# Gated attention and a Hyena block on one Trainium2 core: casts issued one by one behind squares, 64x64 matmuls throughout a batch's Q steps, all engines' orders in one script

## The chip, the cores and the metric

The kernel runs on one core of a Trainium2 chip. The metric is the device time of one execution in microseconds (us). The engines are TensorE (PE, its weight loads PEld), VectorE (DVE), ScalarE (ACT), GpSimd (POOL) and SyncE (SP). POOL and SP mostly issue DMA transfers here.

## The reference

For 8 batches of S = 3136 rows, with u and v of 256 columns and z of 64, all float32:

```python
scores = (1.0 / S) * np.matmul(z, z.transpose(0, 2, 1))
x = u * np.matmul(np.maximum(scores, 0.0) ** 2, v)      # gated attention
...
proj = x @ w_proj                                       # 256 x 768
x1, x2, x3 = proj[..., :D], proj[..., D:2*D], proj[..., 2*D:]
X2 = np.fft.rfft(x2, n=S, axis=1)
H = np.fft.rfft(filter_fft, n=S, axis=0)[None, :, :]
y = x1 * np.fft.irfft(X2 * H, n=S, axis=1) * x3
out = y @ w_out
```

## The kernel before

The inputs are cast to bf16 on their way in; sums are float32 in PSUM.

**Chunks.** The columns of each batch's score matrix are cut into seven chunks (512 five times, 256, 320), 56 chunks in all. A chunk's work on PE is a row of steps. S: scores of a block from zT (`score_mm`, L1650), as two 64-row matmuls at once. ACT (L1808) or DVE (L1810) takes the relu into R_t, and ACT (L1817) or DVE (L1819) squares it into A_t. W and v: the two halves of weighing v_t by A_t into ps_o_t (`by_rows`, L472). The score matrix is symmetric, so some blocks come from earlier chunks' A_t by DMA transposes on SP: M_t, M2e_t and M2o_t (L1757). At a chunk's end DVE multiplies ps_o_t by uT_t into xT_t (the xT eviction, L1861), uT_t being u transposed by SP (L1457).

**Projection and convolution.** A and a are projections, first DFT stages and the like, also through `by_rows`. T is a small table of cosines and sines, made on DVE at the start (gs_t, L811 to L794). Evictions of PSUM by copy are L512 on ACT and L516 on DVE. The convolution is an FFT of length 3136 = 64 x 49. Its middle is the Q steps (`quads`, L1044), sixteen for a batch, whose matmuls are 64x64: forward with S, inverse with TZ, spectra in xh and spec_in_t. B, G and Z steps lead in and out of it (gates in gate_t, products in yT_t, results in ost_t).

**Forms.** A matmul's tile on PE is 64*128 (contraction by output rows) or 64*64; two of the first or four of the second fill the array. `by_rows` and `score_mm` emit 64x128, or two 64x64 in its place when `plan.quarters` is set. Before, `forms()` sets it for an S, W or v that stands between two adjacent Qs of the order, and for Qs.

**Order.** The kernel is unrolled in Python and a `Plan` chooses when each task is emitted. Each engine executes its instructions in the order of emission. PE's order is the string `ORDER`, one letter for a step. Which of ACT and DVE does a relu, square or copy is the string `ENGINES`. All else (what ACT, DVE, SP and POOL do next, which of the three PSUM pairs a step takes, how many fillers PE gets) is decided by `Plan` from assumed costs. Fillers (L674) are matmuls of the identity whose result nobody reads; they keep PE active.

**Casts.** POOL loads the next operands. In each chunk a copy of one element, `await_x` (tick, L561), makes POOL wait for the chunk's xT eviction; then all of that chunk's casts follow: in the first three chunks a third of the filter (xh, L645; the last with its last row, L650, and w_out, L651), z (zn_t, L552), v for the next batch (v_t, L571), and u for two chunks on (un_t, L552). The z and u casts are transposed by SP, `load_uT` (L1457) being added at the xT eviction.

The opening: z of the first batch is loaded (L588), cast into xT_t (L516), transposed on PE (L713), copied to zT_t (L512 or L516), and the first scores follow.

Of the kernel before, what the change touches and what calls it, by code (L numbers as in the profile page):

```python
# [20 lines left out]
NJ = 16  # L21
CHUNKS = (512, 512, 512, 512, 512, 256, 320)
INF = float("inf")
# [4 lines left out]
CLOG = 4.6  # L28
SLOW_TO = 9.0
FILL, SPARE = 0.23, 0.35  # L30
OPENING, AWAKE = 10.5, 7
SPEC_LAG = 1
LATE_F = 3.0
LATE_OUT = 1.5
# [3 lines left out]
TURN = 0.235  # L38
REACH = 2
SHARE = {0: 1, 2: 3}  # L40
SWITCH = 0.096


ORDER = (
    "ASSASSSWWvSAWAWSvSvSvWSWWSvSWvSvWSvWWSvSWvWSvvSSSWSvWWWWWAWavSvAWWSWBvWSvSavWvWSSvvvvvBBaAaaWSWWAWSavWWWAAav"
    "aSWWSWSvvAvavSWSvAWWavSvSvvvBSSWABWavSWWWBSSvavvvBSWWWWaWSWSvvWvvSvASWaSvBvaSWvSWAWWWWWaBWaSvWvWWSvAvvSSavWv"
    "BvaSWvASaSAAaavvSSAaWWWWWWSSvvvWWAASvvaWvWaAvvvQSaWWWSWWWAAavWavWvQWSQvvWSSvWWSvAWavvSvvSvAaSSSWWWSvWvAWvSvW"
    "aSWWWSSvAvavAvWSSWWaWQSvQvvSvQASaWWWSWSSvWAWaWvSvWWSvSSvWSvAvWAWaSvWavSvvvQQAaWSWSvWSAWaWQSvWQWWWSQvSvvvWWQv"
    "QWWvSQvvvvASAaaWWQQvWvSWWSQvWvSWSvWQQvvWvSWQWQWWSvvQvSvAAaaWWQWWSQvAvavSWWSvSvWSvSAvaSWWWWASvSWavSWSvSAvavAB"
    "aaAWWavvWASWaASWaAvvWaBWvaWBWSavvSvSWSBvBaaAWavSBWaWWASvaWASWvWvSWavSWWWSBWSavvWASvavvvvABSaaWWAWaASvaSWAvaA"  # L50
    "WAaaWSvWSvWSvvSAvSaWSWWBSvvWaBWvSavvSSBaSWWWWSWSSvWvvvWSSWBvWWWSSvaWWSBvvaAvaSvSvvAQAaWaWWSWSAWWSavWQvSvvvvS"
    "SSWWWWSWWQvSvAvvvvAaSaWWWQWQvvWQSSWvvWWWQQvWvWSSvSvWWvSQvQvvAAaSaWWWQQWWWSQvSvvSWQWvvWAWavSAvWWWvSvSavvSvAAa"
    "AaWaSWWWWWAWSavSvWQvSvWvvSWQSvvvSAAaSWavWWAWaSvvWWSSSWvWWASvvvSaWWWvWSSvvvAvBSaaWWSWSWWWBSvavSvWSvSWAvaAvSWa"
    "BWSvaAvaAWWaWSBvavAvvaAAaSaWSWWSvBAaaSWvWSSvWSWWASvaWvAvavBSWWavSBvaWWvSSvvABaaWBWWSaSvvWSWBSaWAvaSvvQQvWWWS"
    "WQAvaSvWvABaWaWQvSvQvAASaaWWWSSvWWSvAvaAvQWWQvSWWQvvWvQBaWaWSvWBSvaSvvAAaSaWWQSSvWWSvQQvvWQWWSWQvSvWvAWWSvaA"
    "vSvaQWWSvQvAASaaWWWWSvvSWvSBvWWWSavSvvSWABvSaWaAvaAAaWSavWWSSvWWSWvSSvWBvaWWWSWAWAaWvavvSASavvvvSABaaWWSSvvW"
    "BSWWSavBWWaAvaSvWSvWSAvSWWaWvAvSaSvWvSBvaBAaaSWWAWaWSSWSvWAWaAvavSWBaWSSWvWSvABaSavWvBWaAvSvavSvvBSaSWWQQSvv"
    "WWQvASWvWWaWBQvSaWvSvBWaQvQWWSvWQSvvvBAaaQWWSWQWWSQvWWQvSvQWWvSvWQQvAvaSvAWavAvBaWaSWQvQvAAaSaWWWWWSASvvSvSv"
    "WAaWSWWvaSvvSWWSAvaWBSWavSvBvaSBvaBAaaWAvWWWBSaavvWWSWAvSavvWSAWSaAWavSvSvBASaWWWBaavSWWWSvBvSBaaWWWWSAvaWvW"
    "SBvavvSWvAvAavavBSSaWWWSAvSavWvSSvWWWAAaSavSWvSWSAvAaWSWaSvWBBWaavvSvvSBSaSWWWSWASvvvavSWSWWWAvavSvQWQWWWSWv"  # L60
    "SSvvvvQASaWWQWWWSQvWWWQWQvWSAvSvaAvavvQWSSvWWSvQvSvvAAaSaWWWASaWQvvSQWSvvWQWWWWQWSAvvaWSWQvSvvSvQvvQAAaaSWWW"
    "WAWaSvSWvSvvSWASvavSWWvWASSvWvaWWBSavvvSABaaSWWWWSWWASvWSWaBvvvBaWvSWvaSvvvBASaWaWBvavSWWAWSaWAvavWSAvaWSvWW"
    "SSvWvWWvSAvavvBAaSaWWWASWaSvvWSWSvWSBWvSWaSvBWaWvSAvWSavSWAvSavSvvAAaaBWaSWWWSvWvASvWaWSBvWSavSWvSWWSvSvWWSS"
    "vvBvvaASaAWWWaSvWWSWvvSBvaWSvWSvQSWWWQvvSQvWWvQvvAAaaQWWQvQWSWWAvaWSAWaAWaSvSvvSvvSQWWQWWWSvQvSvAvavAAaaSWWW"
    "BSvavWQvWWQSvvQWSWQvWASvWWSvSavAWWvavvSASaAWWWavWSWWSvvSSvvQvSWWWSWQvvSvASAaaSWWWAWWaSvWWSWvSAWvWSavWvSvvWSv"
    "WvvSvvSASaWSWWWAvaWSWSvWAvSWavWSSvWBvavAvWBaWSavAvvaAWaSvABaaBWSWaAvWaWSAvSaSvWSWvSSvvWWWSAvSWWvSvvaWWSvvSAB"
    "aaBWWWavSWvSWSvSWWBvWaSvWWSvASvWaWSQWSvvQvSvvGAaBaaWWBSvaQWWWQvABvaWSavvQWQSvWWvSSvWWSWvSWQvQvvBAaaWWWSQSvWW"
    "QWWWSWSvWvQvSQvvWvSQvvWQWASvSvvaSAaQWWWWQvvWvWSWSWSWvBWaAvSvavSvvASSaWWWWWASvSaWvvvWWSvAWGvvWWWavWavvAvvaBGa"
    "aAGaaZAaaBGaaBZaaZGaBaaZBaaQQGQQBaQQQaQQBaBQQaQGZQQQaBaQGaGaZBaGaaaBaBaGBaBaaBaBGaBaaBaBGaaBaBBBaaaBa"
)  # L70
# [108 lines left out]
class Plan:  # L179
# [45 lines left out]
    def run(self, task, engine, start):  # L225
# [16 lines left out]
        if engine == "PE" and start < SLOW_TO:  # L242
            cost *= 2
# [1694 lines left out]
```

## Time and profile before

| | us |
|---|---|
| median of 3 runs | 949.24 |
| lowest, highest | 947.19, 952.63 |
| profiled execution | 947.53 |
| its span (first to last instruction) | 945.8 |

The busy shares of the span are PE 97%, DVE 88%, ACT 87%, POOL 21%. A "busy" PE is not PE at its peak: ends of matmuls are modelled, so how far apart the groups start tells more. In rows of a timeline, the bracket at the end is the idle time of the engine before the row and what ended it. The shapes of a matmul row are tile, then what moves through it, and the count after x merges equal neighbours.

### The profile page before, as it was taken

Reading aid. Unit: us, or ns where it says so; the run is one execution under the profiler, and the core shown is the slowest. Engines: PE = TensorE matmul, PEld = TensorE weight load, DVE = VectorE, ACT = ScalarE, POOL = GpSimd, SP = SyncE. Lnnn points to the kernel's source line nnn. Section 1 sums busy time; section 2 is a strip of 40 time slices with the busy share of each in tenths; the row PEclk is TensorE's granted clock in tenths of the full one; section 3 lists DMA queues with packets and bytes.
Section 4 is the critical chain, followed back from the end, with each engine's and each line's share of the span. In section 5 each row is a group of like instructions: output and inputs, shape, how many; then the busy total and the mean of one; then the engine's idle time right before and its main releaser. Section 6 shows DMA issues by size and latency. Waiting matters only on the chain.

```text
span 945.8 us, 29001 instructions
## 1 busy us (share of the span) xinstructions
PE 920.9 (97%) x11990; PEld 544.6 (58%) x11990; DVE 836.6 (88%) x1182; ACT 825.5 (87%) x927; POOL 200.8 (21%) x434
## 2 busy tenths in 40 slices
PE   8998999999999999999999999999999999999986
PEld 3443654557555775557655576556765566555754
DVE  8995699997999999999999779999889988799785
ACT  7785699998899898898989989999899999999672
POOL 5232303122213112212021120312212220001130
PEclk9998999999999999999999999999999999999999
DMA  9999678998999598998799998999899969798867
GB/s 152 152 176 153 146 135 161 176 191 177 181 198 173 110 209 173 207 206 165 156 208 191 204 201 175 183 178 187 173 168 187 190 124 182 172 201 143 210 204 243
DMA packets 321765, 168.40 MB, mean 178 GB/s; under 512 B 231990, under 2 KB 297334, under 8 KB 321632
## 3 DMA queue, kind: packets, MB, share of 16 engines
q1 hardware_dynamic: 290976, 128.39, 66.1%
q0 software_dynamic: 29616, 36.44, 26.1%
q8 instruction: 94, 1.54, 0.7%
q10 hardware_dynamic: 1040, 1.70, 0.6%
q14 instruction: 39, 0.32, 0.1%
HBM read 90.26 MB, written 53.35 MB: 152 GB/s over the span
## 4 chain that ended last, share of the span: by engine, by line
PE 81%; DMA 6%; DVE 6%; ACT 3%; issue 2%; SPq 2%; ACTq 0%; DVEq 0%
PE ps_o_t L472 48%; PE ps_s L472 20%; PE ps_s L1650 10%; PE ps_s L1044 3%; DMA spec<-gs_t 1%; DVE R_t L1810 1%; DMA M2e_t<-A_t 1%; DVE A_t L1819 1%; DMA spec_in_t<-spec 1%; DVE xT_t L1861 1%; ACT R_t L1808 1%; DMA specf<-s_t 1%; DMA ost_t<-in_z_dram 1%; DVE xh L1268 0%; DMA A_t<-spec 0%
## 5 line engine op out<-in xcount | busy, mean ns | idle before, releaser
L472 PE MATMUL ps_o_t<-A_t,v_t 64*128 64x512 bf16 (+4 forms) x4736 | 506.4, 354 | 0.6 <-DVE xT_t L1861 0.4
L472 PEld LDWEIGHTS <-v_t 64*128 64x128 bf16 (+1 forms) x6510 | 295.9, 98 | 209.6 <-PE ps_o_t L472 13.1
L1808 ACT ACTIVATE R_t<-ps_s 128x1024 f32<-128x1024 f32 (+4 forms) x353 | 332.1, 963 | 38.6 <-PE ps_s L1650 29.7
L1817 ACT ACTIVATE A_t<-R_t 128x1024 bf16<-128x1024 f32 (+3 forms) x283 | 276.0, 995 | 22.8 <-DVE R_t L1810 11.0
L1819 DVE TENSOR_TENSOR A_t<-R_t 128x1024 bf16<-128x1024 f32 (+4 forms) x209 | 229.7, 1116 | 15.2 <-ACT R_t L1808 12.8
L1810 DVE TENSOR_SCALAR R_t<-ps_s 128x1024 f32<-128x1024 f32 (+4 forms) x159 | 175.6, 1114 | 27.4 <-PE ps_s L1650 22.4
L1650 PE MATMUL ps_s<-zT_t 64*128 64x512 bf16 (+5 forms) x1209 | 190.9, 353 | 5.8 <-ACT R_t L1808 3.8
L561 POOL COPY tick<-xT_t 1x1 bf16<-1x1 bf16 x54 | 9.6, 178 | 636.5 <-DVE xT_t L1861 636.5
L472 PE MATMUL ps_s<-xT_t,wp 64*128 64x512 bf16 (+2 forms) x864 | 120.3, 349 | 0.5 <-ACT R_t L1808 0.4
L1650 PEld LDWEIGHTS <-zT_t 64*128 64x128 bf16 (+1 forms) x1209 | 68.0, 97 | 50.9 <-issue 6.6
L512 ACT ACTIVATE x_t<-ps_s 128x1024 bf16<-128x1024 f32 (+3 forms) x82 | 76.6, 943 | 19.8 <-PE ps_s L472 18.7
L472 PE MATMUL ps_o_t<-M_t,v_t 64*128 64x512 bf16 (+4 forms) x864 | 93.4, 352 | 0.0
L1861 DVE SCALAR_TENSOR_TENSOR xT_t<-ps_o_t,uT_t 128x256 bf16<-128x256 f32 (+2 forms) x224 | 71.3, 380 | 11.6 <-PE ps_o_t L472 5.8
L1268 DVE TENSOR_TENSOR xh<-xh,H 128x2048 bf16<-128x2048 bf16 x60 | 72.4, 1218 | 1.7 <-ACT xh L512 1.4
L1177 DVE TENSOR_TENSOR gate_t<-ps_s,x_t 128x512 bf16<-128x512 f32 (+2 forms) x106 | 60.6, 613 | 13.2 <-PE ps_s L472 9.0
L1365 DVE TENSOR_TENSOR yT_t<-ps_s,gate_t 128x1024 bf16<-128x1024 f32 (+2 forms) x52 | 56.3, 1087 | 12.7 <-PE ps_s L472 10.7
L472 PE MATMUL ps_s<-wp,xT_t 64*128 64x256 bf16 x800 | 65.3, 269 | 0.4 <-DVE s_t L516 0.2
L472 PEld LDWEIGHTS <-wp 64*128 64x128 bf16 x896 | 47.4, 94 | 30.2 <-issue 3.6
L552 POOL DMA_DIRECT2D un_t<-in_u_dram x112 | 59.7, 552 | 10.2 <-issue 6.8
L472 PE MATMUL ps_s<-wo,yT_t 64*128 64x256 bf16 x756 | 60.6, 270 | 0.9 <-DVE yT_t L1365 0.6
L571 POOL DMA_DIRECT2D v_t<-in_v_dram x112 | 58.8, 541 | 8.2 <-issue 7.0
L472 PE MATMUL ps_o_t<-M2e_t,v_t 64*128 64x512 bf16 (+2 forms) x440 | 52.0, 353 | 1.6 <-DVE xT_t L1861 1.5
(176 smaller groups left out, 881.0 us busy)
## 6 DMA issues: line engine op xcount, KB each, us to landing
out_dram<-ost_t SPq DMA_DIRECT2D x58, 256.0 KB
spec_in_t<-spec SPq DMA_DIRECT2D x56, 192.0 KB
spec<-gs_t SPq DMA_DIRECT2D x56, 192.0 KB
v_t<-in_v_dram POOLq DMA_DIRECT2D x80, 128.0 KB, 5.0
un_t<-in_u_dram POOLq DMA_DIRECT2D x80, 128.0 KB, 5.5
spec<-s_t SPq DMA_DIRECT2D x40, 256.0 KB
conv_in_t<-spec SPq DMA_DIRECT2D x34, 256.0 KB
out_dram<-ost_t POOLq DMA_DIRECT2D x10, 256.0 KB, 3.7
```

The costliest lines, as they stand in the source:

```text
L472: last = matmul(o[ds(i, n)], w[:, ds(i, n)], m, **kw)
L512: nc.scalar.activation(out_, in_, AF.Copy)
L552: nc.gpsimd.dma_start(out=t[ds(j * N1, N1), lo - t0 : hi - t0, :], in_=x[:, n2 : n2 + hi - lo, :])
L571: nc.gpsimd.dma_start(out=t[ds(j * N1, N1), ds(v_at(a), (b - a) * D)], in_=r[:, n2 + a - lo : n2 + b - lo, :].rearrange("p t d -> p (t d)"),)
L1177: nc.vector.tensor_tensor(g[:, :, ::-1] if h == 0 else g, p, x, ALU.mult)
L1268: nc.vector.tensor_tensor(x, x[:, 1].unsqueeze(1).to_broadcast([P, 2, 2, 2 * D]), h, ALU.mult)
L1650: matmul(o[ds(m, n)], zt[h, ds(t * P + m, n)], q, start=True, stop=True)
L1808: nc.scalar.activation(r, p, AF.Relu)
L1810: nc.vector.tensor_single_scalar(r, p, 0.0, ALU.max)
L1817: nc.scalar.activation(a, r, AF.Square)
L1819: nc.vector.tensor_tensor(a, r, r, ALU.mult)
L1861: nc.vector.scalar_tensor_tensor(x[:, ::-1] if h == 0 else x, f, inv_s2, ut, ALU.mult, ALU.mult)
```

## The change

One string, `SCRIPT`, replaces `ORDER`, `ENGINES` and the planner's costs. It holds PE's steps in order (a digit behind the letter for the PSUM pair and for which of the waiting tasks), and between them c, d, s and p with a number: the next task of ACT, DVE, SP and POOL by its place among the tasks that wait. `F` with two digits is that many fillers (second, in base 36) into a pair (first).

```diff
+SCRIPT = (
+    "d4d4d0d4F0oA00d4d3F12S1c0d2S2c2d2d2d2A00c3c2d3d2F13Wc1c1S1d0S2d2d1Wc0A00p0c0d1S1S2c1d1Wd1A00c0Wd2S1s0c0vd1S2"
...
```

The first line holds `F0o`, 24 fillers, ahead of the first transposes (`A00`). Eight more stand ahead of all, as before. Fillers are 44 in all (32 before): 8, 24, 2, 3 and, at the end, 7; before they were 8, 3, 4 and, at the end, 17.

The form of PE's tiles goes by spans, from the first to the last of a batch's sixteen Qs:

```diff
+    def spans(self, steps):
+        at = [i for i, x in enumerate(steps) if x[0] == "Q"]
+        cuts = [0, *range(len(at) % NJ, len(at) + 1, NJ)]
+        got = [False] * len(steps)
+        for a, b in zip(cuts, cuts[1:]):
+            for i in range(at[a], at[b - 1] + 1):
+                got[i] = True
+        return got
...
+        for (k, *x), self.quarters in zip(steps, self.spans(steps)):
```

In the built order the matmuls on PE grow from 11990 to 14133, and the places where neighbours differ between 64x128 and 64x64 fall from 92 to 20. DVE has 176 relus and ACT 336 (159 and 353 before), and of the copies DVE has 8 more and ACT 8 fewer.

The casts wait for squares and not for the xT eviction. A chunk's casts are put into `due`, and one is released behind each of the squares 1 to 5 of the next chunk, in the order u, v, z, filter; where POOL takes a released cast is set by `SCRIPT`. The filter comes in six parts (three before), v's cuts move by a row group, and `load_uT` is added with its cast:

```diff
+PACE = (1, 2, 3, 4, 5)
...
-    def await_x(xt):
-        nc.gpsimd.tensor_copy(tick[:], xt["t"][0:1, 1, 0:1])
+    def await_q(un):
+        tc.add_manual_dep(
+            nc.gpsimd.nop().ins, squares[un].ins.name, mybir.DependencyInfo(needs, reason.DATA), reason="paces the casts",
+        )
...
-    filt_cuts = ((0, 8), (8, 16), (16, NT))
+    filt_cuts = ((0, 4), (4, 8), (8, 12), (12, 16), (16, 20), (20, NT))
...
-            got.append(go_u)
+                load_uT(*slots[x], [])
+
+            got.insert(0, go_u)
+        got += late_
...
+        at_ = [u_ for u_ in scored if u_[:2] == un[:2]].index(un)
+        if at_ in PACE and due:
+            due.pop(0)(on("POOL", lambda un=un: await_q(un), 0.1, [q_]))
...
-            calls = casts_at(b, c)
-            if calls or b == 0 and c < 3:
-                tick_ = on("POOL", lambda xt=xt: await_x(xt), 0.1, [x_])
...
+            assert not due, (b, c, len(due))
+            due += casts_at(b, c)
```

POOL issues 378 DMAs for 356 before; SP's DMAs are as many as before. The line numbers shift by about 90 (by_rows 472 to 376, fillers 674 to 580, casts of u and z 552 to 456, of v 571 to 477, of the filter 645 to 551, M transposes 1757 to 1673).

How the instructions move, at three places. First DVE in the opening, from the first cast of z. Before (gs_t is the table T in the making, ps_s_139 the pair with the transposed z):

```order
L516 CAST xT_t<-ost_t 128x4x64 x2
L811 TENSOR_SCALAR gs_t<-yT_t,percol 128x32 x4
L812 TENSOR_SCALAR gs_t<-yT_t,percol 128x1
L813 TENSOR_SCALAR gs_t<-yT_t,percol 128x1
L789 TENSOR_SCALAR gs_t<-gs_t 128x128
L790 TENSOR_SCALAR gs_t<-gs_t 128x128
L516 CAST xT_t<-ost_t 128x8x64 x2
L794 SCALAR_TENSOR_TENSOR gs_t<-gs_t 128x128
L1810 TENSOR_SCALAR R_t<-ps_s_141 128x1024
L516 COPY zT_t<-ps_s_139 128x1024
```

After:

```order
L420 CAST xT_t<-ost_t 128x4x64 x2
L420 COPY zT_t<-ps_s_139 128x512
L717 TENSOR_SCALAR gs_t<-yT_t,percol 128x32 x4
L718 TENSOR_SCALAR gs_t<-yT_t,percol 128x1
L719 TENSOR_SCALAR gs_t<-yT_t,percol 128x1
L695 TENSOR_SCALAR gs_t<-gs_t 128x128
L696 TENSOR_SCALAR gs_t<-gs_t 128x128
L420 CAST xT_t<-ost_t 128x8x64
L700 SCALAR_TENSOR_TENSOR gs_t<-gs_t 128x128
L1726 TENSOR_SCALAR R_t<-ps_s_141 128x1024
L420 COPY zT_t<-ps_s_139 128x1024
```

The first zT eviction came from ACT and is now DVE's, ahead of the steps for T; one of the casts of 128x8x64 went to ACT.

Second POOL, at the casts of the third chunk of the first batch. Before:

```order
L561 COPY tick<-xT_t 1x1
L645 DMA xh_120<-in_moe_filter_fft_dram 64x8x256
L645 DMA xh_120<-in_moe_filter_fft_dram 64x2048
L649 MEMSET gate_t 64x256
L650 DMA gate_t<-in_moe_filter_fft_dram 64x256
L651 DMA wo_205<-in_moe_w_out_dram 128x2x256
L571 DMA v_t<-in_v_dram 64x1024 x2
L552 DMA un_t<-in_u_dram 64x1024 x2
L552 DMA zn_t<-in_z_dram 64x256 x2
L552 DMA zn_t<-in_z_dram 64x512
```

After (the waits for squares stand between them and are not among these rows):

```order
L456 DMA un_t<-in_u_dram 64x1024 x2
L477 DMA v_t<-in_v_dram 64x1024
L477 DMA v_t<-in_v_dram 64x256
L477 DMA v_t<-in_v_dram 64x1024
L477 DMA v_t<-in_v_dram 64x256
L551 DMA xh_120<-in_moe_filter_fft_dram 64x4x256
L551 DMA xh_120<-in_moe_filter_fft_dram 64x1024
L456 DMA zn_t<-in_z_dram 64x256 x2
L456 DMA zn_t<-in_z_dram 64x512
L551 DMA xh_120<-in_moe_filter_fft_dram 64x4x256
L551 DMA xh_120<-in_moe_filter_fft_dram 64x1024
L555 MEMSET gate_t 64x256
```

The burst behind one tick has become five releases, u first, with the filter in two parts (its last row and w_out follow). On SP around the same place, M2e_t before and after:

```order
L1757 DMA_TRANSPOSE M2e_t<-A_t 128x8x128
L1521 DMA_TRANSPOSE zT_t<-zn_t 128x4x128
L961 DMA spec_0_59<-s_t 128x4x256
L1457 DMA_TRANSPOSE uT_t<-un_t 128x8x128
L1757 DMA_TRANSPOSE M2e_t<-A_t 128x8x128
```

```order
L1673 DMA_TRANSPOSE M2e_t<-A_t 128x8x128
L1673 DMA_TRANSPOSE M_t<-A_t 128x8x128 x2
L1673 DMA_TRANSPOSE M2e_t<-A_t 128x8x128
L867 DMA spec_0_59<-s_t 128x4x256
L1363 DMA_TRANSPOSE uT_t<-un_t 128x8x128
```

The second M2e_t no longer stands behind a uT_t transpose, and the two M_t transposes stand between the two.

Third PE, behind a Q step in the middle of the kernel. Before:

```order
L1044 MATMUL ps_s_141<-spec_in_t,S_218 64x512
L472 LDWEIGHTS T_216
L472 MATMUL ps_s_139<-x_t,T_216 128x512
...
L472 LDWEIGHTS v_t
L472 MATMUL ps_o_t<-A_t,v_t 128x512
```

After:

```order
L950 MATMUL ps_s_140<-spec_in_t,S_218 64x512
L376 LDWEIGHTS T_216
L376 MATMUL ps_s_141<-x_t,T_216 64x512
...
L376 LDWEIGHTS v_t
L376 MATMUL ps_o_t<-A_t,v_t 64x512
```

The step behind the Q, and the weighing behind it, keep 64 output rows inside the span; before, the wide form came back at once.

More of the change, by code (lines that the diff above doesn't have):

```diff
@@ L264, in run @@
+    def run(self, task, engine):
+        task.emit(engine)
         for kid in task.kids:
-            for d, extra in kid.deps:
-                if d is task:
-                    kid.ready = max(kid.ready, end if extra == ISSUED else end + lat + (extra or 0.0))
             kid.left -= 1
```

363 lines of the change are left out of this document (133 added, 230 removed).

## The prediction

> **What bounds the kernel now.** I read the page first, then a table of stretches, then TensorE's timeline inside them. A run is told from no change when it moves by more than about 0.5% (4.7 us).
>
> ```profile
> span 945.8 us, 29001 instructions
> PE 920.9 (97%) x11990; PEld 544.6 (58%) x11990; DVE 836.6 (88%) x1182; ACT 825.5 (87%) x927; POOL 200.8 (21%) x434
> ...
> PE   8998999999999999999999999999999999999986
> ...
> PEclk9998999999999999999999999999999999999999
> ```
>
> TensorE (PE) is busy for 97% of the span, and the slices show where it is not: the first two, the fourth (the clock dips there too) and the last two. The stretches say the same in us (columns: length, then busy PE, PEld, DVE, ACT, POOL, granted clock, DMA share, GB/s).
>
> ```profile
> 12.00:30.00 18.00, 15.43 (x141) 6.41 (x138) 17.75 (x22) 16.59 (x18) 5.10 (x11) 1.00 1.25 152
> 60.00:70.00 10.00, 9.57 (x92) 4.03 (x89) 9.03 (x19) 9.38 (x10) 4.99 (x10) 1.00 1.09 140
> 70.00:80.00 10.00, 6.62 (x48) 2.76 (x46) 4.86 (x5) 3.83 (x4) 1.56 (x3) 0.77 1.41 166
> 80.00:90.00 10.00, 8.90 (x73) 4.04 (x71) 7.03 (x10) 5.49 (x6) 3.35 (x8) 0.88 0.79 133
> 100.00:850.00 750.00, 746.74 (x9849) 449.62 (x9849) 680.21 (x930) 688.32 (x774) 150.59 (x325) 1.00 0.95 178
> 900.00:946.00 46.00, 35.13 (x578) 21.79 (x572) 31.81 (x37) 24.97 (x27) 10.15 (x19) 0.96 0.73 221
> ```
>
> From 100 to 850 us PE idles 3.3 us of 750. There only less work on PE, or the same work at a better pace, saves time. Elsewhere a wait that goes is a gain, if nothing else ends late behind it. A delay of the opening reaches the end undiminished, since the long middle has no slack to take it up.
>
> **Part 1: the form spans.** A change between 64x128 and 64x64 matmuls is seen as a longer step from one group to the next (columns: start, length, engine, line, operation, tiles, shape, count).
>
> ```profile
> 303.75 0.61 PE L472 MATMUL ps_o_t<-A_t,v_t 64*128 64x512 bf16 x4
> 304.19 0.61 PE L472 MATMUL ps_o_t<-M2e_t,v_t 64*128 64x512 bf16 x4
> 304.73 0.41 PE L1044 MATMUL ps_s<-xh,TZ 64*64 64x512 bf16 x4
> 304.97 0.39 PE L1044 MATMUL ps_s<-spec_in_t,S 49*64 49x512 bf16 x4
> 305.19 0.60 PE L472 MATMUL ps_o_t<-M_t,v_t 64*64 64x512 bf16 x8
> 305.62 0.60 PE L472 MATMUL ps_o_t<-A_t,v_t 64*64 64x512 bf16 x8
> ...
> 309.07 0.39 PE L1044 MATMUL ps_s<-spec_in_t,S 49*64 49x512 bf16 x4
> 309.39 0.39 PE L472 MATMUL ps_o_t<-A_t,v_t 64*128 64x512 bf16 x2
> ```
>
> Start to start, four 64x128 matmuls take 0.44 us (303.75 to 304.19), and eight 64x64 ones 0.43 (305.19 to 305.62): the forms work at one pace. Into the Q step the four take 0.54 (304.19 to 304.73), so the change costs about 0.11. A Q group takes 0.22 between neighbours of its own form (304.97 to 305.19) and 0.32 into the wide form (309.07 to 309.39): 0.10. Another place reads higher, or has a record missing:
>
> ```profile
> 525.54 0.61 PE L472 MATMUL ps_o_t<-A_t,v_t 64*128 64x512 bf16 x3
> 526.08 0.41 PE L1044 MATMUL ps_s<-xh,TZ 64*64 64x512 bf16 x4
> ```
>
> 0.54 for three, 0.33 of work: 0.21. I take 0.11, the lower rows' value, since four in 0.54 would give the same. The instructions in order have 92 changes before and 20 after. Of these 74 and 17 lie between the places of 110 and 880 us, so 57 fewer: 57 x 0.11 = -6.3 us (bounds 57 x 0.10 = -5.7 and 57 x 0.21 = -12.0). The 2143 more matmuls are halves of wide ones and cost nothing at the pace above; the cover is that two run side by side. Some 38 groups of eight have only 128 columns, a case not in this trace: by columns 0.108 us each (a quarter of 0.43), at worst twice that, so 0 to +4.1; I take 0, the value to which 512 columns are nearest.
>
> This rests on the weight loads staying hidden:
>
> ```profile
> L472 PEld LDWEIGHTS <-v_t 64*128 64x128 bf16 x4538 | 234.0, 94 | 170.5 <-issue 13.0 <-PE ps_o_t L472 11.8 <-DVE xT_t L1861 9.4
> L472 PEld LDWEIGHTS <-v_t 64*64 64x64 bf16 x1972 | 62.0, 106 | 39.1 <-PE ps_o_t L472 1.3 <-PE ps_s L1044 1.0 <-DVE xT_t L1861 0.2
> ```
>
> A narrow load takes 106 ns for half the columns, a wide one 94: dearer, but beside the matmuls in both. The Trainium skill (TensorEngine Tiling (Array Packing), Restrictions) says that column tiling disables the fast weight load, which speaks against longer spans. The 106 ns agree with it in sign; the equal pace says that it is not felt.
>
> **Part 2: the casts.** The worst place of the kernel is one burst of them.
>
> ```profile
> 62.69 0.18 POOL L561 COPY tick<-xT_t 1x1 bf16<-1x1 bf16 x1 [10.82 <-DVE xT_t L1861]
> 63.15 1.23 POOL L645 DMA_DIRECT2D xh<-in_moe_filter_fft_dram  x2 [0.29 <-issue]
> ...
> 65.90 1.06 POOL L571 DMA_DIRECT2D v_t<-in_v_dram  x2
> 66.92 1.08 POOL L552 DMA_DIRECT2D un_t<-in_u_dram  x2
> ```
>
> Behind one xT eviction POOL queues the last third of the filter, then v, u and z. The chain of waits and the timeline go on:
>
> ```profile
> 63.93 10.68 DMA M2e_t<-A_t
> ...
> 74.69 1.06 ACT L1817 ACTIVATE A_t<-R_t 128x1024 bf16<-128x1024 f32 x1 [4.80 <-DMA M2e_t<-A_t]
> ...
> 76.71 0.58 PE L1650 MATMUL ps_s<-zT_t 64*128 64x512 bf16 x1 [3.38 <-ACT R_t L1808]
> 76.72 4.84 PE L472 MATMUL ps_o_t<-A_t,v_t 64*128 64x512 bf16 x20
> ...
> 86.96 1.28 PE L472 MATMUL ps_o_t<-M2e_t,v_t 64*128 64x512 bf16 x8 [1.04 <-DVE xT_t L1861]
> ```
>
> A transpose of squares that falls among these transfers is under way for 10.68 us. ScalarE's next square waits 4.80 for its buffer, the relu stands behind that square, and PE waits 3.38 for the relu. Then twenty matmuls take 4.84 us where 20 x 0.108 = 2.16 would do, at a granted clock of 0.77 and 0.88: 2.7 more. A last wait is 1.04. At stake: 3.38 + 2.68 + 1.04 = 7.1 us.
>
> After the change u comes first in that chunk, each cast stands behind its own early square, and the filter comes in halves among v and z. Both M2e transposes of the place now stand ahead of the next uT transpose on SP; before, the second stood behind one. But the same bytes move in about the same 10 us (squares 1 to 5 of a chunk surround the xT eviction), and M_t transposes come later in SP's queue. I take -5.0 of 0 to -7.1. The late thing next would be an M_t transpose, with the same form of wait.
>
> By the Trainium skill (TensorE: Matmul & The Clock Gate, Part 1) an idle gap of a window of about 3.4 us halves the clock. The 3.38 of wait with 0.77 behind it agree; by that rule a wait merely shortened to 2 us would give back 1.4 of itself and all 2.7 of the clock, -4.1.
>
> The other effects of this part are costed at 0. The 54 tick copies become POOL nops; 22 more DMAs at about 0.6 us of issue (1.23 for two) are 13 us on POOL. The cover is its idleness:
>
> ```profile
> L561 POOL COPY tick<-xT_t 1x1 bf16<-1x1 bf16 x54 | 9.6, 178 | 636.5 <-DVE xT_t L1861 636.5
> ```
>
> 636.5 us of waiting ahead of the ticks. A nop that waits for a square holds the next casts behind it, then SP's uT transpose and z's, needed about a chunk later; if that cover were gone, one late uT costs a wait like the 1.04 at 86.96. Load_uT issued earlier on SP moves uT ahead of some M transposes: 0, up to one such wait in each of a few chunks, which is inside the bounds of the stall.
>
> **Part 3: the opening.**
>
> ```profile
> 1.72 3.59 PE L674 MATMUL ps_s<-ident 128*128 128x512 bf16 x8 [1.72 <-DVE tick L598]
> ...
> 5.55 0.79 DVE L811 TENSOR_SCALAR gs_t<-yT_t,percol 128x32 f32<-128x32 int32 x4
> 5.69 0.61 PE L713 MATMUL ps_s<-ident,xT_t 128*128 128x128 bf16 x4 [0.37 <-DVE xT_t L516]
> ...
> 7.39 0.61 PE L1650 MATMUL ps_s<-zT_t 64*128 64x512 bf16 x4
> ...
> 9.18 0.68 DVE L516 COPY zT_t<-ps_s 128x1024 bf16<-128x1024 bf16 x1
> ...
> 9.92 0.82 PE L1650 MATMUL ps_s<-zT_t 64*128 64x512 bf16 x6
> ...
> 923.93 2.12 PE L674 MATMUL ps_o_t<-ident 128*128 128x512 bf16 x9
> ```
>
> Eight fillers at the slow clock take 3.59, the last of them 0.6 to its end: 0.43 apart. Nine at the full clock take 2.12: 0.21 apart. The clock is full by the scores at 7.39 (0.61 for four, as at 303.75). After the change 32 fillers stand ahead of the first transposes: 13 x 0.43 from 1.72 is 7.3, and 19 x 0.21 more is 11.3. The transposes start there and not at 5.69, though their data is there at 5.6. The first zT eviction moves from ScalarE to VectorE, ahead of the sine steps (from 5.55 in the rows), which so start near 12.2. From 5.55 to the second scores at 9.92 are 4.4 us, giving 16.6 and a lag of 6.7. The waits of 12 to 30 us (18 - 15.43 = 2.6) may take up part; I take +5.0, bounds +3.0 and +6.7.
>
> **Part 4: the tail and the engines.** After 900 us PE idles 10.9 of 46 and others end its waits. There 15 changes (1.65) and 10 fillers (2.1) are fewer, mostly inside waits: 0 to -3.8, taken -1.3. VectorE gets 17 more relus and 8 more copies, ScalarE as many fewer:
>
> ```profile
> L1810 DVE TENSOR_SCALAR R_t<-ps_s 128x1024 f32<-128x1024 f32 (+4 forms) x159 | 175.6, 1114 | 27.4 <-PE ps_s L1650 22.4
> ```
>
> 25 x 1.11 = 28 us more work on VectorE, 22 of them between 100 and 850. The cover is its idleness there, 750 - 680.2 = 69.8, of which 22.4 us in this row alone wait for PE: 0, with the case where the cover fails among the rivals.
>
> **The sum.** +5.0 - 5.0 - 6.3 - 1.3 = -7.6 on a profiled span of 945.8, so 938.2. That execution took 947.53, so 939.9; it was 1.7 below the median 949.24, which gives 941.6 for the median. I say 941, the full form saving being the lower of its readings. The bounds of the parts make it 922 to 954; both ends need all terms on one side.
>
> **Rivals.**
> - The stall stays, or moves to an M_t transpose: the filter's bytes are the same. For it speaks the DMA share of 1.41 in 70 to 80; against it that M2e leaves ahead of the casts. 941 + 5 = 946.
> - The opening is not felt: if the 2.6 us of waits from 12 to 30 and later small ones take up most of it, 941 - 4 = 937. Against it: PE is the last to be late from 100 on.
> - The changes of form are not what costs, the first load of a new kind of tile is: then 57 fewer give nothing, 947. Against it: within the Q spans tiles alternate too, at 0.22.
> - Slower: VectorE becomes the bound. From 100 to 850 it would have 702 us of work in about 743, idle 41. If its order needs more idle than that, PE waits for relus. At 55 idle the stretch is 757 and the time 955; at today's 69.8, 772 and 970. Against it speaks that its idle time is mostly ended by PE.
> - Slower: the narrow loads are felt in the longer spans. 2143 wide matmuls become 4286 narrow ones; at 12 ns each, two side by side, +26: 967. The equal pace at 305 speaks against it.
>
> **How the numbers follow.** Forecast 0.50 (own range 935 to 946), stall stays 0.15, opening not felt 0.13, VectorE 0.12, forms not the cost 0.07, loads felt 0.03. Faster (below 944.5): 0.43 of the forecast, 0.05 of the stall, 0.13, 0.02 of the forms: 0.63. Slower (above 954): three quarters of VectorE and the loads, 0.11. The rest, 0.26, is the same. The range 932 to 956 leaves out about 0.03 below and 0.11 above.
>
> **What would show it.** First scores near 13 and second near 16.6 in the opening; no PE wait of 3 us and no clock below 0.95 from 60 to 90; about 20 changes of form at 0.1; PE idle from 100 to 850 still under 5 us, VectorE near 94% there. I am wrong if PE waits for R_t or xT_t in the middle, if the early squares hold casts so long that uT is late, or if 64x64 passes in the spans run slower than 0.43 for eight.

## The result, and the profile after

The changed kernel takes 985.27 us (four runs, 981.45 to 990.31) against 948.76 for the kernel before on the same chip: a ratio of 1.038, 95% interval 1.031 to 1.045. The forecast was 941, so it is wrong in sign, and the time lies outside the range. The profiled run has a span of 988.5 us, 42.7 more than before. Below, the time of a run is the median of its executions in the fast state, where the record tells a slow one too.

The page of the kernel after (busy time, then the slices of TensorE and of its granted clock):

```profile
span 988.5 us, 33292 instructions
...
PE 933.5 (94%) x14133; PEld 604.5 (61%) x14133; DVE 858.8 (87%) x1205; ACT 808.8 (82%) x904; POOL 203.2 (21%) x402
...
PE   7999899899999999998998999899999899999976
...
PEclk9999999899999999999998999999999899999999
```

The dip of the fourth slice is gone. In its place six 8s stand in the middle, where before had none, and at three of them the clock dips as well. The stretches (length, then busy PE, PEld, DVE, ACT, POOL, clock, DMA share, GB/s) give the amounts:

```profile
12.00:30.00 18.00, 14.40 (x114) 6.40 (x114) 16.36 (x27) 13.54 (x18) 3.88 (x8) 0.91 1.32 159
60.00:70.00 10.00, 9.83 (x102) 4.79 (x98) 9.92 (x11) 7.67 (x8) 2.20 (x4) 1.00 1.25 191
70.00:80.00 10.00, 9.21 (x85) 4.10 (x85) 9.90 (x14) 6.00 (x7) 7.45 (x14) 1.00 1.14 170
80.00:90.00 10.00, 9.60 (x87) 4.16 (x83) 9.82 (x17) 6.59 (x9) 4.66 (x9) 1.00 1.30 209
100.00:850.00 750.00, 718.80 (x11195) 475.09 (x11196) 659.92 (x909) 638.71 (x713) 146.23 (x284) 0.98 0.95 168
900.00:988.50 88.50, 72.89 (x1335) 51.69 (x1323) 67.04 (x92) 55.37 (x67) 15.53 (x30) 0.97 0.71 197
```

From 60 to 90 us TensorE (PE) is busy 28.64 of 30, before 25.09, and at the full clock. From 100 to 850 it idles 31.2 us where before it idled 3.3, at a clock of 0.98. VectorE is idle for 90 us there: it is no bound.

The two traces can also be compared at the same work (columns of matmuls done by PE, fillers left out). The kernel after is 7.5 us behind at 30 us of before, 8.2 at 70, 1.6 at 100, 41.2 at 850 and 42.7 at the end. So 39.6 us of the loss arise in the long middle, which the prediction had called closed to waits. They are 28.1 us more idle time (31.4 against 3.3 over that work) and some 12.5 of the clock: the trace has it at half for five stretches, 30.7 us in all, in 24.9 of which PE works. What is left of PE's busy time, taken at the full clock, is 745.8 us after and 746.7 before.

One stall of the middle, from the timelines of SP's queue, POOL, PE and ScalarE, in order of time:

```profile
527.40 5.19 SPq L1673 DMA_TRANSPOSE M_t<-A_t  x2
...
527.49 1.04 POOL L456 DMA_DIRECT2D un_t<-in_u_dram  x2 [12.42 <-ACT A_t L1733]
531.17 1.04 POOL L477 DMA_DIRECT2D v_t<-in_v_dram  x2 [2.64 <-ACT A_t L1733]
...
531.54 1.06 PE L376 MATMUL ps_o_t<-M2o_t,v_t 64*64 64x512 bf16 x16 [0.47 <-DVE xT_t L1780]
...
534.85 1.06 ACT L1733 ACTIVATE A_t<-R_t 128x1024 bf16<-128x1024 f32 x1 [3.30 <-DMA M_t<-A_t]
...
537.57 1.92 PE L376 MATMUL ps_o_t<-M_t,v_t 64*64 64x512 bf16 x16 [4.11 <-DMA M_t<-A_t]
```

SP issues two M_t transposes. The u cast, released by a square, starts 0.1 us behind the first, and v follows. ScalarE's square waits 3.30 us for its buffer, PE 4.11 us for the transposed block, and then sixteen matmuls take 1.92 us that took 1.06 six us earlier: the half clock. The chain of waits names the transfer; it holds ten M transposes of over 4.5 us from 100 to 900 us, of which these are three:

```profile
456.32 8.11 DMA M_t<-A_t
...
528.89 8.63 DMA M_t<-A_t
...
633.52 7.85 DMA M_t<-A_t
```

Before, the chain holds none from 100 us on; the one at 63.93 was the only one of that length on it. With three shorter ones, M transposes make 78.5 us of the chain after; by an estimate that is some 30 more than 13 undisturbed ones would take (3.73 us each, from the count further below). SP itself stands longer too. Its waits for the casts that it has to transpose (total us, times, longest), after:

```profile
SPq L1363 <- DMA un_t<-in_u_dram: 97.6, 34, 10.2
...
SPq L1427 <- DMA zn_t<-in_z_dram: 21.0, 12, 4.0
```

and before:

```profile
SPq L1457 <- DMA un_t<-in_u_dram: 17.1, 7, 6.6
```

### The profile page after: what moved, and what is told of

Same layout as the page of the kernel before. It is cut to its first block, busy times and chain, and to the rows that moved or that the text cites. A ratio compares the mean times of both kernels' runs of the same rounds, so it can differ in the third digit from the quotient of the medians.

```text
span 988.5 us, 33292 instructions
## 1 busy us (share of the span) xinstructions
PE 933.5 (94%) x14133; PEld 604.5 (61%) x14133; DVE 858.8 (87%) x1205; ACT 808.8 (82%) x904; POOL 203.2 (21%) x402
## 4 chain that ended last, share of the span: by engine, by line
PE 72%; DMA 10%; DVE 9%; ACT 4%; issue 3%; SPq 1%; POOL 0%; DVEq 0%; ACTq 0%; POOLq 0%
PE ps_o_t L376 43%; PE ps_s L376 16%; PE ps_s L1566 9%; DMA M_t<-A_t 7%; PE ps_s L950 3%; ACT R_t L1724 2%; DVE A_t L1735 2%; DVE R_t L1726 1%; DMA M2e_t<-A_t 1%; PE ps_s L580 1%; DVE xT_t L1780 1%; DVE xh L1174 1%; ACT A_t L1733 1%; DMA spec<-s_t 1%; ACT x_t L416 1%
## 5 line engine op out<-in xcount | busy, mean ns | idle before, releaser
L376 PE MATMUL ps_o_t<-A_t,v_t 64*64 64x512 bf16 (+5 forms) x5522 | 516.3, 358 | 1.9 <-ACT A_t L1733 0.5
L376 PEld LDWEIGHTS <-v_t 64*64 64x64 bf16 (+1 forms) x7622 | 333.7, 102 | 193.7 <-issue 14.9
L1724 ACT ACTIVATE R_t<-ps_s 128x1024 f32<-128x1024 f32 (+2 forms) x336 | 316.3, 960 | 73.6 <-PE ps_s L1566 62.6
L1735 DVE TENSOR_TENSOR A_t<-R_t 128x1024 bf16<-128x1024 f32 (+3 forms) x213 | 233.6, 1115 | 18.8 <-ACT R_t L1724 14.1
L1726 DVE TENSOR_SCALAR R_t<-ps_s 128x1024 f32<-128x1024 f32 (+2 forms) x176 | 194.9, 1119 | 32.1 <-PE ps_s L1566 20.2
L1566 PE MATMUL ps_s<-zT_t 64*64 64x512 bf16 (+5 forms) x1420 | 199.3, 358 | 14.3 <-DVE R_t L1726 4.7
L376 PE MATMUL ps_s<-xT_t,wp 64*64 64x512 bf16 (+5 forms) x1148 | 124.1, 355 | 1.8 <-DVE xT_t L1780 0.8
L376 PE MATMUL ps_o_t<-M_t,v_t 64*64 64x512 bf16 (+5 forms) x1016 | 101.7, 362 | 11.2 <-DMA M_t<-A_t 11.2
L376 PE MATMUL ps_s<-wp,xT_t 64*128 64x256 bf16 (+1 forms) x1056 | 66.3, 270 | 0.3 <-DVE R_t L1726 0.2
L1271 DVE TENSOR_TENSOR yT_t<-ps_s,gate_t 128x1024 bf16<-128x1024 f32 (+2 forms) x49 | 53.3, 1092 | 11.3 <-PE ps_s L376 9.1
L376 PE MATMUL ps_s<-wo,yT_t 64*128 64x256 bf16 (+1 forms) x832 | 58.6, 272 | 0.8 <-ACT M2e_t L416 0.3
```

Of the source, the lines that this page charges most:

```text
L376: last = matmul(o[ds(i, n)], w[:, ds(i, n)], m, **kw)
L1566: matmul(o[ds(m, n)], zt[h, ds(t * P + m, n)], q, start=True, stop=True)
L1724: nc.scalar.activation(r, p, AF.Relu)
L1726: nc.vector.tensor_single_scalar(r, p, 0.0, ALU.max)
L1735: squares[un] = nc.vector.tensor_tensor(a, r, r, ALU.mult)
```

## The experiments

The theories named in the expectations: **A**, SP stands at a uT or zT transpose whose cast is late, and the M_t transposes behind it start late. **B**, casts and M transposes are now in flight together, and the transposes take longer. **C**, the fixed order of the script is to blame. **D**, PE got faster by the spans and runs into its operands.

**The parts alone.** `b_spans` is the kernel before with the form spans, `b_casts` with the casts' part of the diff (await_q, PACE, six filter parts, load_uT with its cast) under the old planner, `b_both` with both. The edit for the spans, then the core of that for the casts:

```diff
-        forms = self.forms()
+        forms, spans, narrow = self.forms(), self.spans(), False
...
+            self.parts, narrow, self.quarters = narrow, forms[self.at], spans[self.at]
```

```diff
-            calls = casts_at(b, c)
-            if calls or b == 0 and c < 3:
-                tick_ = on("POOL", lambda xt=xt: await_x(xt), 0.1, [x_])
...
+            assert not due, (b, c, len(due))
+            due += casts_at(b, c)
```

> The kernel before with the change's spans of 64x64 tiles and nothing else; every engine's order stays that of before. If a change of form costs 0.11 us on a PE that is never waited for: 72 fewer, -5 to -8 us, 938 to 943. If a faster or differently shaped PE overtakes its operands (new theory D: PE is slower by the form changes and the waits are where it catches up): 946 to 960, with new PE waits for M_t or R_t inside the Q steps.

> The kernel before with the change's casts alone (squares release them one by one, filter in six parts, uT with its cast); its planner still sets the orders of ACT, DVE, SP and POOL. Theory A (SP held at uT by a late cast): SP waits for un_t of 60 us or more and PE waits for M_t, 965 to 985. Theory B (collisions of paced casts with M_t transposes): flights of M_t up from 4.2 to 4.8 us, 965 to 985, too. If the casts are harmless and the script alone costs the time: 940 to 950, without the 3.4 us wait at 73 us.

> The kernel before with spans and casts: all of the change but the script of orders, engine choices, pairs and fillers. If the script costs the time: 935 to 950. If casts and spans cost it: 975 to 990, as the changed kernel less its opening (some 6 us).

Measured: spans 1.0066 (1.0029 to 1.0103), casts 1.0394 (1.0324 to 1.0464), both 1.0399 (1.0351 to 1.0447). The casts' part makes a loss of the whole size without any script, so C is not needed for it. It is not the casts' time alone, though: in `b_casts` the old planner also sets the order of SP, and in part of DVE and ACT, anew. The spans alone lose a little: the stretch of `b_spans`, in an execution of 963.02 us (median 956.13), shows PE idle 19.7 us where before it was 3.3.

```profile
100.00:850.00 750.00, 730.31 (x11427) 475.15 (x11424) 662.28 (x908) 673.13 (x756) 148.40 (x320) 1.00 0.98 174
```

**Forms and opening undone in the kernel after.** `a_forms` has the rule of before for 64x64 (118 changes of form, 11766 matmuls); `a_f0` has no 24 fillers in the opening.

```diff
-        at = [i for i, x in enumerate(steps) if x[0] == "Q"]
...
+            if k in "SWv":
+                waiting.append(i)
+                continue
+            for j in waiting:
+                got[j] = last == k == "Q"
+            got[i] = k == "Q"
```

```diff
-    "d4d4d0d4F0oA00d4d3F12S1c0d2S2c2d2d2d2A00c3c2d3d2F13W
+    "d4d4d0d4F00A00d4d3F12S1c0d2S2c2d2d2d2A00c3c2d3d2F13W
```

> The changed kernel with the rule of before for 64x64 (an S, W or v between two adjacent Qs): 118 changes of form in place of 20. A and B: the spans save 98 x 0.11 to 0.15, so this is slower by 8 to 14 us where PE is the last, 990 to 998. If the spans were what made the kernel slower: 960 to 975.

> The changed kernel without the 24 fillers ahead of the first transposes. If a delay of the opening reaches the end: -5 to -7 us, 978 to 981, first scores near 7.5 us. If later waits take it up: within 2 us of 985.

Measured: `a_forms` 975.16 us, 1.0265 (1.0218 to 1.0313); `a_f0` 973.8 us (two executions, 969.45 and 978.16), 1.0271 (1.0194 to 1.0349). The longer spans gain nothing in this kernel, they rather lose some 10 us; on `b_casts` they cost nothing (1.0394 to 1.0399). Without the fillers it is some 10 us less by the ratios, with intervals that overlap (1.0312 to 1.0451 for the kernel after); at 30 us of before, the trace of `a_f0` is 1.5 us behind where that of the kernel after is 7.5.

**SP's place (A).** `a_nopace` takes the waits for squares away (the casts go as soon as POOL reaches them); `a_utlate` holds each uT transpose back for four SP places.

```diff
-        tc.add_manual_dep(
-            nc.gpsimd.nop().ins, squares[un].ins.name, ...
-        )
+        pass
```

```diff
+                if getattr(task, "later", False):
+                    held.append([task, HOLD_UT])
+                    continue
...
+        t.later = (b, c) > (0, 1)
```

> The changed kernel (985 us) with the POOL waits for squares left out: casts go as soon as their buffers are free; all orders stay. Theory A (SP stands at a uT or zT transpose whose cast a square has held back, and the M_t transposes behind it start late): SP's waits for un_t fall from 97.6 us to under 35, the waits of PE for M_t and the long R_t waits mostly go, time 955 to 965 us. Theory B (casts and M_t transposes collide in the DMA engines, SP's waiting is harmless): the collisions stay, 978 to 990. Theory C (the fixed order itself is late, whatever the casts): 980 to 988.

> The changed kernel with each uT transpose put four places later in SP's queue; the squares hold the casts as before. A: SP's waits for un_t fall below 40 us though the casts land no earlier, M_t starts earlier, 958 to 970 us. B: the same transfers at the same times, 980 to 988. C: 980 to 988.

Measured: 999.89 us, 1.0547 (1.0459 to 1.0634), and 1012.32 us, 1.0652 (1.0571 to 1.0734). Both are slower than the kernel after, and outside of what any of the three theories gave. In `a_nopace` SP hardly waits for u any more:

```profile
SPq L1361 <- DMA un_t<-in_u_dram: 6.5, 2, 6.2
```

The 97.6 us of waiting went and the time rose by some 15 us: A is not what costs the most. In `a_utlate` SP's wait for u falls to 11.4 us while PE's waits for M_t grow from 11.2 to 21.4; why holding uT back costs 26 us stays open.

**The casts' place in time (B).** `a_tick` puts the waits back at the xT eviction and lets a chunk's casts go together, with the script otherwise kept. `b_notick` does the reverse to the kernel before: the 54 tick copies are left out, so that casts go earlier, while PE, DVE, ACT and SP keep their exact order. The edits of `a_tick` and of `b_notick`:

```diff
-            nc.gpsimd.nop().ins, squares[un].ins.name, mybir.DependencyInfo(needs, reason.DATA), reason="paces the casts",
+            nc.gpsimd.nop().ins, evicts_[key].ins.name, mybir.DependencyInfo(needs, reason.DATA), reason="paces the casts",
```

```diff
     def await_x(xt):
-        nc.gpsimd.tensor_copy(tick[:], xt["t"][0:1, 1, 0:1])
+        pass
```

> The changed kernel with one thing undone: POOL's waits end at the chunk's xT eviction again (all casts of the chunk then follow at once, still u, v, z, filter, in the change's parts); casts that the script has earlier are held until then, and a uT or zT transpose that needs one stands where its cast is. Script, spans and fillers stay. Theory B (casts of the squares overlap with the M_t transposes that are issued in the 4 us ahead of an eviction): casts in flight during an M_t transpose fall from 1.6 to about 0.7, its flight from 4.7 to about 4.2, time 950 to 962. Theory A (SP held back at uT): 960 to 985, since uT waits for its cast as long as before. If the script is to blame: 980 to 990.

> The kernel before, POOL's 54 waits for the xT eviction left out and nothing else: the orders of PE, ACT, DVE and SP are the same to the row. Casts go as soon as their buffers are free, so u and z can be late for no uT or zT transpose. Theory A alone (a late cast holds SP): no slower, 940 to 950, SP's 17 us for un_t gone. Theory B (casts beside M_t transposes): casts in flight during an M_t transpose up from 0.6 to over 1.2, 960 to 985.

Measured: `b_notick` 978.41 us, 1.0361 (1.0292 to 1.0430). A shift of the casts in time and nothing else costs some 30 us. But M_t is not what PE waits for most there (3.6 us in all, the longest 1.4). Its three longest waits (7.6, 6.7 and 5.4 us) stand behind other transfers of SP, those of the spectra. From the chain:

```profile
51.73 10.81 DMA specf<-s_t
...
171.16 10.27 DMA spec_in_t<-spec
...
556.41 11.39 DMA spec<-gs_t
```

Beside these, 4.4, 1.8 and 6.2 casts are under way as a mean. At the same work `b_notick` is 13 us behind by 60 us of before, 7 at 100, 17 at 200, 29 at 600 and 28 at 880. So the shift of the casts is shown to cost, at a few places and through other transfers of SP too; B's picture of M transposes in every chunk is not what this run shows.

`a_tick` took 1027.89 us, 1.0838 (1.0783 to 1.0893), against B alone, which would have had it recover: uT and zT transposes stand at the script's early places while their casts are late again.

```profile
SPq L1383 <- DMA un_t<-in_u_dram: 214.9, 54, 7.9
```

Here A does cost. `a_tick_ut` moves each uT six SP places later:

```diff
+        t.later = HOLD_UT if (b, c) > (0, 1) else 0
```

> The changed kernel with both theories' causes undone: casts behind the xT eviction (as a_tick) and each uT transpose six places later in SP's queue, so that its cast has landed. Script, spans and the 32 fillers of the opening stay. A and B together: SP's waits for un_t from 215 us to under 40, casts beside M_t as in a_tick (0.7), time 950 to 962 (before, plus some 6 of the opening). If the script is to blame: 975 or more.

It took 1008.54 us, 1.0598 (1.0536 to 1.0660): some 20 us back, with the wait for u down to 7.2 us and one of 70.6 for z in its place. Two more runs tried to carry z along, without the 24 fillers. In the first the copies of VectorE stood right behind the held zT transposes; the second moved them too.

```diff
+                t.later = HOLD_ZT
...
+                    t.later = HOLD_X
```

> The changed kernel with its casts released behind the xT eviction as before, and with what this displaces moved too: each uT and each zT transpose six SP places later (the copies behind a zT go with it), and without the 24 fillers. All else is the script's order. SP then neither carries the M transposes beside the casts nor stands in front of a late cast. If the casts' place, SP's place and the opening are the whole loss, it comes back to between 945 and 960 us. If the fixed order itself costs (an order found for one timing of the casts doesn't bear another), SP's waits for un_t and zn_t fall from 78 us to under 20 and the time stays above 975: about 1008.5 less 4 for the fillers and some 7 for the zn_t waits on the chain, 995 to 1000.

> a_tick_utz_f0 without its fault (there VectorE's copies behind a zT stood right behind the transpose and waited 94.5 us for it): each uT six SP places later, each zT four, and the copies behind a zT eight VectorE places after it. Casts behind the xT eviction, no 24 fillers, all else the script's order. If place of the casts, SP's standing and the opening are the whole loss, 945 to 960 us. If the script's order bears only the timing of the casts it was written for, above 975, with waits of TensorE on other things than M transposes.

They took 1087.71 us, 1.1453 (1.1410 to 1.1495), where VectorE waited 94.5 us for zT, and 997.67 us, 1.0481 (1.0415 to 1.0547). In the second, SP's waits for u and z are 12.8 and 6.0 us, and the time does not come back. So this script with casts at the xT eviction stays slow in each form tried. Whether the script does it, or the places that uT and zT were moved to (in `a_utlate` such a move alone cost 26 us), and whether the script has a part in the loss of the changed kernel itself, these runs leave open.

**The casts' bytes (B).** `a_nov` is the kernel after without the v casts of batches 2 to 7; batch 1's v is weighed in their place, and 9.8 MB of 36.4 on POOL's queue are not moved. `b_nov` is the same edit on the kernel before, the control, and `b_casts_nov` on `b_casts`.

```diff
                     def gv():
+                        if n > 1:
+                            v16[n] = v16[1]
+                            return
```

> The changed kernel without v's casts for the batches 2 to 7 (they weigh batch 1's v again; it leaves out 9.6 MB of 36 MB of casts), the waits of POOL kept. B: fewer casts beside M_t, the later five batches lose half of their new waits, 965 to 975. A: SP's waits for u and z go down by little, 980 to 988. Script to blame: 982 to 988.

> The control to a_nov: the kernel before without the v casts of batches 2 to 7 (batch 1's v is weighed instead, 9.6 MB are not moved), all else as it was. If the casts' bytes cost only where they meet the transposes, TensorE is the bound here as before and the time is the same, 944 to 949 us. If fewer bytes help any version alike, it gains the 26 us that a_nov gained on the changed kernel: 923.

> b_casts (the kernel before with the change's casts alone, 986.7 us) without the v casts of batches 2 to 7. If it is the casts' bytes in their new place that make the transposes late, it comes back as a_nov did, to 950 to 960 us. If the pacing itself costs (POOL's place, the waits for squares, uT issued with its cast), the bytes do not matter and it stays above 975.

Measured: `a_nov` 959.30 us, 1.0111 (1.0077 to 1.0146); `b_nov` 943.88 us, 0.9966 (0.9940 to 0.9991); `b_casts_nov` 970.68 us, 1.0247 (1.0191 to 1.0304). The same bytes are worth 26 us after the change and 4 before it (948.0 - 943.9). So some 22 us of the loss (the intervals of the ratios allow 14 to 30) hang on where v's casts lie, and not on how many there are; their bytes and POOL's time to issue them go together here. In `a_nov` SP still waits nearly as long as in the kernel after, and most of the loss is gone, which speaks against A once more:

```profile
SPq L1363 <- DMA un_t<-in_u_dram: 85.7, 34, 7.5
```

On `b_casts` they are worth some 14 us of 37 by the ratios; the other 23 are in neither theory, and the new order of SP, DVE and ACT is a rival for them that no run takes apart. The stretch of `b_casts_nov` has PE idle 19.9 us still, spread over waits for relus and spectra:

```profile
100.00:850.00 750.00, 730.15 (x9541) 447.39 (x9539) 658.98 (x903) 671.50 (x752) 91.29 (x178) 1.00 0.84 159
```

Counted over every M_t transpose that starts between 110 and 880 us (from the row of its issue to its landing, and the u, v and z casts under way beside it, as a mean over its flight):

| | casts beside one | mean flight, us | time, us |
|---|---|---|---|
| before | 0.62 | 4.17 | 948.8 |
| b_nov | 0.29 | 3.70 | 943.9 |
| b_spans | 0.67 | 4.48 | 956.1 |
| a_nov | 0.78 | 4.17 | 959.3 |
| b_casts_nov | 0.48 | 3.89 | 970.7 |
| a_forms | 1.40 | 4.40 | 975.2 |
| b_notick | 1.08 | 4.44 | 978.4 |
| after | 1.59 | 4.61 | 985.3 |
| b_casts | 1.32 | 4.40 | 986.7 |
| a_nopace | 1.74 | 4.95 | 999.9 |
| a_tick | 0.74 | 4.09 | 1027.9 |

In the kernel after, the 34 transposes with less than a quarter of a cast beside them take 3.73 us, the 40 with one or more 5.41 (before 3.71 for 49, and 4.80 for 17). So a transpose beside casts is longer: that part of B is shown. That the longer flights are the loss is not: in `a_tick` both columns came down as B wanted and the time rose, `b_casts_nov` has shorter flights than before and takes 22 us more, and flights of 7 us and more were there before too (six, nine after) without PE waiting for them. Whether the change also took away the room in which a long one did no harm is not shown.

**The stall of before from the other side.** In `b_filt` the last third of the filter goes behind the v, u and z casts of its burst, and POOL waits for the M2e transpose ahead of it.

```diff
+            if not self.behind:
+                self.wait_m2e()
+                self.last_part.emit("POOL")
```

> The kernel before with one thing moved: the last third of the filter, its last row and w_out go behind the v, u and z casts of the same burst, and POOL waits for the M2e transpose of the 73-us stall before it issues them. If the casts' bytes beside that transpose are what makes it 10.68 us long, it falls to 5 to 7, ScalarE's wait of 4.80 and TensorE's of 3.38 shrink to under 1, the dip of the clock goes, and the time falls by 3 to 6 us, to 943 to 946. If the M_t pair that follows on SP now collides with the filter, a wait of 2 to 4 us stands some 5 us later and the time is the same within 0.5%.

Measured: 946.16 us, 0.9983 (0.9952 to 1.0015), the same. The transpose still takes 9.02 us with the filter out of its way (10.68 before). From the chain:

```profile
64.13 9.02 DMA M2e_t<-A_t
```

The clock's dip is gone, but PE idles 1.46 us there and 2.66 between 80 and 90, where it idled 1.10. So the filter is not what makes that transpose long, against the expectation of 5 to 7 us, and the stall moved on; v, u and z still start beside it. No run here is faster than the kernel before with all of its work.

## Why the prediction was wrong, point by point

**The opening, +5.0, was right in its mechanism and a little small.** From the timelines of PE and DVE:

```profile
1.72 9.96 PE L580 MATMUL ps_s<-ident 128*128 128x512 bf16 x32 [1.72 <-DVE tick L504]
...
11.94 0.42 DVE L420 COPY zT_t<-ps_s 128x512 bf16<-128x512 bf16 x1 [6.32 <-PE ps_s L619]
...
12.42 0.60 PE L1566 MATMUL ps_s<-zT_t 64*128 64x512 bf16 x4
...
16.21 0.60 PE L1566 MATMUL ps_s<-zT_t 64*128 64x512 bf16 x4
```

The fillers end at 11.68 (forecast 11.3), the second scores start at 16.21 (16.6), 6.3 us after those of before. By 30 us nothing of it had been taken up: the kernel after was 7.5 us behind, 6 of which go without the 24 fillers (`a_f0`, 1.5).

**The stall at 73 us, -5.0, was right.** PE does 3.55 us more from 60 to 90, the clock dip is gone, and at the same work 6.6 us come back between 70 and 100 us of before. The rival that it stays fell.

**The forms, -6.3, did not reach the time.** Over the same work (PE's own progress from 100 to 800 us of it) the steps at changes of form cost about 9 us at some 65 places before and 2 at 14 after, so the price of 0.11 a change was near. But PE's busy time for the work of 100 to 850 us, at the full clock, is 746.7 us before, 745.8 after and 745.2 in `b_spans`: the 7 us do not show in the sum, and what takes their place is open. And `b_spans` is 0.7% slower, with 17 us more of idle time over that work. The prediction read the 3.3 us of idle as "There only less work on PE, or the same work at a better pace, saves time", and did not ask what the other engines and SP had to spare. That PE idles more with the spans is shown; that it does so because it got faster, as D has it, is not.

**The step that failed** is the end of Part 2: "The other effects of this part are costed at 0." Its reasons were the idleness of POOL and uT's distance, and the price of a lost cover "up to one such wait in each of a few chunks". What stood at 0 was the largest term: the casts' part of the change, with the orders that the old planner makes of it, costs 3.9% (`b_casts`, some 37 us), a shift of the casts with all other orders kept some 30 us (`b_notick`), and v's casts are worth 26 us in their new place and 4 in the old. The wait came, but at other transfers than uT. Releasing casts at squares 1 to 5 puts them in the stretch of a chunk where SP issues its M transposes, in nearly every chunk. Counted over the trace from 100 to 880 us: before, 99 of the 100 u casts start within 5 us behind an xT eviction, where 1 to 4 M_t transposes start in each us of that distance; from 8 to 2 us ahead of an eviction it is 5 to 10 in each. After, 80 of 95 u casts and 70 of 111 v casts start ahead of the eviction. The prediction had this very collision in its rows, as the 10.68 us of the one stall, and used it only to price that stall's going; "The late thing next would be an M_t transpose" stands there, with the price of one stall and not of one at many places. Against the span of before, at the same work: +8.2 up to 70 us with the opening, -6.6 with the stall, +39.6 in the middle and +1.5 behind it make the 42.7.

How the new place becomes waits is shown in part: in the kernel after PE's longest waits for M_t stand behind transposes of 5.8 to 8.6 us with casts beside them, while `b_notick` loses at the spectra. That the sum of the middle is such collisions, and not also the script, is argued.

**The tail, -1.3, did not come.** From 946 on PE idles 12.8 us by the stretches (15.6 from 900, less 2.9 up to 946), against 10.9 from 900 on before; the last 96 us of before took 1.5 more.

**The rivals.** VectorE as the bound (955 to 970) had the right side for the wrong reason: it is busy 659.9 of 750. Narrow loads are not felt: eight 64x64 matmuls step in 0.43 us inside the spans, as at 305 us before. No rival held a collision of casts and transposes in the middle. Of the signs named at the end, "if PE waits for R_t or xT_t in the middle" came true for R_t, behind squares that wait for M_t.

**What stays open:** why a transpose is longer beside casts. The Trainium skill (DMA: Bandwidth & Descriptors, Queues, rings and completion order) says that a DMA engine takes turns between its queues, packet by packet. The 3.73 and 5.41 us agree with it in sign; no run here separates sharing of the engines from SP's time to issue. Open too are the 23 us of `b_casts` that v's casts don't explain.

## What to carry to other kernels

The place in time of background loads is part of a tuned schedule. Ask of each load that moves which transfers will be in flight beside it, in every repetition of the loop, and do not put it at 0 because its one visible stall goes. The worst stall times the repetitions is no price either: 7.1 us in some 54 chunks would be 383, and 43 were lost. A run of the kernel before with the loads alone moved, as `b_notick`, prices such a move. And an idle share near zero on the engine that is the bound says who is late last, not by how much the next one is early.

## What the runs showed of the hardware

A wait of TensorE of 2.37 us was followed by the half clock; waits of 2.00 and 1.85 were not. The rows of PE in the kernel after, then two stretches that contain such waits (clock third from the end):

```profile
121.87 0.41 PE L950 MATMUL ps_s<-spec_in_t,S 49*64 49x512 bf16 x4 [2.00 <-ACT R_t L1724]
...
641.41 0.63 PE L376 MATMUL ps_o_t<-M_t,v_t 64*64 64x512 bf16 x8 [2.37 <-DMA M_t<-A_t]
641.87 0.39 PE L1566 MATMUL ps_s<-zT_t 64*64 64x512 bf16 x4
...
642.57 1.08 PE L376 MATMUL ps_o_t<-A_t,v_t 64*64 64x512 bf16 x8
```

```profile
120.00:125.00 5.00, 3.13 (x81) 2.69 (x84) 4.82 (x6) 3.85 (x6) 0.00 (x0) 1.00 0.63 138
...
640.00:645.00 5.00, 3.58 (x44) 1.77 (x48) 2.00 (x2) 2.43 (x3) 0.00 (x0) 0.75 1.45 121
```

The first matmuls after the wait still run at full speed (0.39 for four); about a us later eight take 1.08 where 0.60 is usual, until 645.9. The Trainium skill (TensorE: Matmul & The Clock Gate, Part 1) puts the drop behind an idle window of about 3.4 us. The waits of 4.11 above and 4.46 at 787.69 agree; the one of 2.37 does not. The length of a wait alone does not decide it: in `b_casts` one of 1.65 us was followed by a clock of 0.50 (104.4 to 107.8 us), in `a_utlate` one of 2.82 was not (1.00 from 586 to 592 us). So in these traces a wait of 1.6 to 2.9 us may or may not have half clock behind it. In the middle of the kernel after, each stretch at half lasts 3.4 or 6.8 us.
